# Sliding-window attention and a two-layer MLP on one core: token tiles of 512 instead of 384, with four accumulator banks, the activation kept in PSUM and fixed places for the attention

## The chip, the core and the metric

The kernel runs on one core of a Trainium2 chip. The metric is the device time of one execution in microseconds, as the median of the runs. A core has five engines with a queue each, which this text calls by the profile's names: PE (TensorE, the matrix array; PEld is its loading of weights), DVE (VectorE), ACT (ScalarE), POOL (GpSimd) and SP (SyncE, which here only issues DMAs). SBUF is the working memory of 128 partitions. PSUM is the memory that PE writes; it has eight banks, each holding 512 float32 values in each partition. [...]

## What is computed

```python
def _attn_ref(q, k, v):                    # B, H, S, D = 8, 8, 576, 64
    scores = 1.0 / np.sqrt(D) * np.matmul(q, k.transpose(0, 1, 3, 2))
    rel = pos[:, None] - pos[None, :]
    mask_plain = (rel >= 0) & (rel < 32)                     # heads 0 to 3
    mask_dil = (rel >= 0) & (rel < 128) & (rel % 4 == 0)     # heads 4 to 7
    ...
    attn = softmax of the masked scores
    return np.matmul(attn, v)

def _moe_ref(x, w_in, w_out):              # 4608 tokens, 512 -> 2048 -> 512
    h = x @ w_in
    g = np.where(h >= 1, h, np.where(h <= -1, 0.0, (h + 1) ** 2 / 4))
    return g @ w_out
```

The attention's output, 8 batches of 576 tokens with 8 heads side by side, is the input `x` of the MLP. All data is float32.

## The kernel before

**Precision.** PE multiplies one float32r term by another at one pass. The kernel splits most operands into a high and a low part and adds three products (high by high, low by high, high by low), so each float32 product of the MLP is three matmuls. `xh`/`xl`, `gh`/`gl` and the two halves of `wi` and `wo` are such parts.

**The MLP.** It walks over NT = 12 tiles of TOK = 384 tokens and, in each, over 16 blocks `f` of 128 hidden units. One pair (tile, f) is a step, 192 in all. `layer1(t, f)` runs 12 matmuls (four 128-row chunks of `x` by three terms) of 384 columns into a PSUM tile with the tag `h` (two buffers). Then comes the activation: ACT computes relu(h/2 + 1/2) into `y` in SBUF (L365), DVE multiplies min(y, 1) by y (L366) and takes the maximum with `h` (L367), which is the last reader of `h`; ACT rounds `y` to `gh` (L370), and DVE, or POOL in the first 11 steps of tile 0, computes `gl = y - gh` (L372). `layer2(t, f)` (L385) runs 9 matmuls of 512 columns: three 128-token blocks, each with an accumulator bank `acc0` to `acc2` of its own that is open over all 16 steps, times three terms. After f = 15 the three banks are copied out, two by ACT and one by DVE, and stored.

**The attention.** A query tile is 96 rows and sees 128 keys, six such tiles to a head. The 16 heads of batches 0 and 1 are *native*: `scores` (L187) multiplies unsplit float32, which the trace shows as two matmuls for each query tile, and the heads of a pair lie in partitions 0 to 63 and 64 to 127. `reduce` on DVE (L158) adds the mask and takes the maximum, `softmax` runs six exponentials on ACT (L233), a sum and a reciprocal on DVE (L241, L244) and one multiplication on POOL (L245). `transpose_pe` (L280, L282) turns a native head's weights by PE and copies them out of PSUM, four query tiles by ACT and two by DVE. `values(n, part)` (L313) multiplies a pair of heads by `v` and writes `xh` and `xl` (L298 on ACT, L299 on DVE). The other 48 heads are split: `split` makes high and low parts on ACT and POOL (L134 to L139), `scores_split` (L208) scores two query tiles at a time; ACT copies the low half out of PSUM (L216), POOL adds the mask (L226), and DVE reduces (L158). Their transposes run on DVE (L255).

**Banks.** PSUM's eight banks are `acc0` to `acc2`, two of `h` and three of `att`, which serves scores, transposes and values. While no MLP work runs, batch 0 uses the `acc` and `h` banks too.

**Order.** PE's queue is written out by hand. First all of batch 0's attention runs, then `partial` does the first chunk of layer 1 for `early` = 5 blocks, and then the steps follow: each step `s` issues `layer1(s)`, then `layer2(s - 2)`, and between or behind them units of attention. Over tile 0 these are the eight heads of batch 1 from the list `units`, spread evenly; later `pattern` gives the split heads six steps for each pair, from step 15 on, so 24 pairs fill 144 steps. On the other engines a scheduler orders the instructions by their place in the program, with the priorities raised around batch 0. The weights arrive as 64-bit numbers and are converted while tile 0 runs: two operations on ACT (L111, L117 or on DVE L119), one on DVE (L122), a rounding on ACT (L127) and a subtraction on POOL (L128) for each of 32 blocks; `issue_after` ties their pace to the activation two steps back. Tile 1 needs all of batch 1, so its first step stands behind that batch's attention. DMAs are issued by SP in the order of the program: `load_pair`, `load`, `load_values` and `fetch`.

Of the kernel before, what the change touches and what calls it, by code (L numbers as in the profile page):

```python
# [27 lines left out]
QT, NQ = 96, 6  # L28
KPAD = S + 32
CLS = S // DIL  # L30
TOK = 384
# [8 lines left out]
def body(ctx, tc, q, k, v, mask, eye, w_in, w_out, out):  # L40
# [63 lines left out]
    def weights(f, w, name):  # L104
# [22 lines left out]
        nc.scalar.copy(out=w[f][:, 0], in_=mf)  # L127
# [16 lines left out]
    banks = [("acc0", 1), ("acc1", 1), ("acc2", 1), ("h", 2), ("h", 2)]  # L144
# [24 lines left out]
    def scores(n, t0, t1):  # L169

        hd = heads[n]
        plain = n % H < H // 2
        if t0 == 0:
            begin(n)
        if n < H:
            tag, bufs = banks[(2 * n + t0 // 4) % len(banks)]
        else:
            tag, bufs = "att", 3
        sp = ps.tile([128, 512], F32, tag=tag, name=f"s{n}_{t0}", bufs=bufs)
        sv = sp[:QT, : (t1 - t0) * 128].rearrange("p (t j) -> p t j", j=128)  # L180
        if n == 0 and t0 == 0:

            half = half_t.broadcast_to([128, 128])
            for _ in range(11):
                PE.matmul(out=sp[:, :128], lhsT=half, rhs=half, start=True, stop=True)
        for t in range(t0, t1):
            PE.matmul(  # L187
                out=sv[:, t - t0],
                lhsT=hd["qs"][:, t * QT : (t + 1) * QT],
                rhs=hd["ks"][:, t * QT : t * QT + 128],  # L190
                start=True,
                stop=True,
            )
        for t in range(t0, t1):
            which = (0 if t == 0 else 2) if plain else t % 3
            reduce(n, t, (sv[:, t - t0], msk[:, which]))

    def scores_split(n, t0):
# [6 lines left out]
        sp = ps.tile([128, 512], F32, tag="att", name=f"s{n}_{t0}", bufs=3)  # L205
# [53 lines left out]

    def borrow_pts():  # L260

        for i in range(2):
            for part in ("xh", "xl"):
                both = pool.tile([128, NC * TOK], F32, tag=part, name=f"pts_{part}{i}", bufs=4)
                for j in range(2):
                    pt = both[:, j * NQ * QT : (j + 1) * NQ * QT]
                    first_pts.append(pt.rearrange("p (t j) -> p t j", j=QT))

    first_pts = []

    def pt_of(n):
        return first_pts[n] if n < H else pts[n % 2]

    def transpose_pe(n):
        pt, c = pt_of(n), heads[n]["c"]
        for t0, t1 in ((0, 4), (4, NQ)):
            tag, bufs = banks[(2 * n + t0 // 4) % len(banks)] if n < H else ("att", 3)
# [3 lines left out]
            copy = nc.scalar.copy if t0 == 0 else nc.vector.tensor_copy  # L281
# [4 lines left out]
    def xtile(t):  # L286
        if t not in xt:
            xt[t] = (
                pool.tile([128, NC, TOK], F32R, tag="xh", name=f"xh{t}", bufs=4),
                pool.tile([128, NC, TOK], F32R, tag="xl", name=f"xl{t}", bufs=4),  # L290
            )
        return xt[t]
# [10 lines left out]
    def values(n, part):  # L303

        b, h = divmod(n, H)
        plain = h < H // 2
        odd = b % 2
        first = (2 if odd else 4) if plain else 3
        t0, t1 = ((0, first), (first, NQ))[part]
        op = ps.tile([128, 512], F32, tag="att", name=f"o{n}_{part}", bufs=3)  # L310
        for j in range(2):
            for t in range(t0, t1):
                PE.matmul(  # L313
                    out=op[64 * j : 64 * j + 64, (t - t0) * QT : (t - t0 + 1) * QT],
                    lhsT=heads[n + j]["vt"][:, t],
                    rhs=pt_of(n + j)[:, t],
                    start=True,
                    stop=True,
                )
        c = h // 2  # L320
        tok0 = b * S
        if plain:
            w = (t1 - t0) * QT
            tok = tok0 + t0 * QT
            t, at = divmod(tok, TOK)
            store_x(op[:, :w], t, c, lambda x: x[:, at : at + w])
        else:
            cut = CLS * (TOK // 2 if odd else TOK) // S
            for a, z in ((0, cut), (cut, CLS)):
                t, at = divmod(tok0 + DIL * a, TOK)  # L330
                store_x(
                    op[:, : 2 * CLS].rearrange("p (r i) -> p r i", r=2)[:, :, a:z],
                    t,
                    c,
                    lambda x: x[:, at : at + DIL * (z - a)].rearrange("p (i r) -> p r i", r=DIL)[
                        :, 2 * part : 2 * part + 2
                    ],
                )
# [6 lines left out]
    def layer1(t, f, cs=range(NC), bank=("h", 2)):  # L345
        xh, xl = xtile(t)
        if cs[0] == 0:
            hps[t, f] = ps.tile([128, 512], F32, tag=bank[0], name=f"h{t}_{f}", bufs=bank[1])[:, :TOK]
# [14 lines left out]
        gh = pool.tile([128, TOK], F32R, tag="gh", name=f"gh{t}_{f}", bufs=3)  # L363
        gl = pool.tile([128, TOK], F32R, tag="gl", name=f"gl{t}_{f}", bufs=3)
        nc.scalar.activation(out=y, in_=hp, func=AF.Relu, bias=half_t, scale=0.5)  # L365
        nc.vector.scalar_tensor_tensor(out=y, in0=y, scalar=1.0, in1=y, op0=ALU.min, op1=ALU.mult)  # L366
        activated = nc.vector.tensor_tensor(out=y, in0=hp, in1=y, op=ALU.max)  # L367
        if t == 0:
            last["g", f] = activated
        nc.scalar.copy(out=gh, in_=y)  # L370
        low = nc.gpsimd if t == 0 and f < 11 else nc.vector
        low.tensor_tensor(out=gl, in0=y, in1=gh.bitcast(F32), op=ALU.subtract)  # L372
# [4 lines left out]
    def layer2(t, f):  # L377
        gh, gl = gs.pop((t, f))
        for m in range(TOK // 128):
# [24 lines left out]
    units = []  # L404

    slots = {}

    def plan_rest():

        pattern = [("0", "1"), ("2", "VW"), ("", ""), ("T3", "4"), ("5", ""), ("U", "")]  # L410

        def after(m):
            if m < nhead - 1:
                split(m + 1)
            if m < nhead - 2:
                load(m + 2)
            softmax(m)

        for p in range((nhead - native) // 2 + 1):
            n = native + 2 * p  # L420
            ops = {"V": [lambda n=n: values(n - 2, 0)], "W": [lambda n=n: values(n - 2, 1)]}
            if n < nhead:
                for j in range(2):
                    for i, u in enumerate(score_units(n + j, after)):
                        ops[str(3 * j + i)] = [u]
                ops["T"] = [lambda n=n: (transpose(n), load_values(n))]
                ops["U"] = [lambda n=n: transpose(n + 1)]
            for i, (a, b) in enumerate(pattern):
                if p == 0 and i < 3:
                    continue  # L430
                s = NF + 6 * p + i - 3
                lists = slots.setdefault(s, ([], []))
                for names, l in ((a, lists[0]), (b, lists[1])):
                    for x in names:
# [211 lines left out]
```

## Time and profile before

| what | us |
|---|---|
| median of 3 runs | 976.36 |
| the profiled execution, its own time | 976.49 |
| span of its trace, first to last instruction | 974.7 |
| mean granted TensorE clock over the span | 0.981 |
| DVE busy | 707.2 (73%) |
| ACT busy | 537.5 (55%) |
| POOL busy | 428.7 (44%) |

Of the three runs one took 2337 us and the other two lie 0.16 us apart; the median is one of those two. The profiled execution takes 1.8 us more than its span. A row of groups reads: line, engine, operation, output<-inputs, shape, count | busy us, mean ns of one | idle time of that engine before them, and what ended it. A row of windows reads: the window, its length, and for each engine the time that it is busy and its count of instructions. A row of the timeline or of the chain reads: start, duration (both us), engine, line, tiles, count, and in square brackets the wait in front with what ended it.

### The profile page before, as it was taken

Reading aid. Unit: us, or ns where it says so; the run is one execution under the profiler, and the core shown is the slowest. Engines: PE = TensorE matmul, PEld = TensorE weight load, DVE = VectorE, ACT = ScalarE, POOL = GpSimd, SP = SyncE. Lnnn points to the kernel's source line nnn. Section 1 sums busy time; section 2 is a strip of 40 time slices with the busy share of each in tenths; the row PEclk is TensorE's granted clock in tenths of the full one; section 3 lists DMA queues with packets and bytes.
Section 4 is the critical chain, followed back from the end, with each engine's and each line's share of the span. In section 5 each row is a group of like instructions: output and inputs, shape, how many; then the busy total and the mean of one; then the engine's idle time right before and its main releaser. Section 6 shows DMA issues by size and latency. Waiting matters only on the chain.

```text
span 974.7 us, 15838 instructions
## 1 busy us (share of the span) xinstructions
PE 950.1 (97%) x5398; PEld 847.6 (87%) x5398; DVE 707.2 (73%) x1922; ACT 537.5 (55%) x1609; POOL 428.7 (44%) x375
## 2 busy tenths in 40 slices
PE   8879989999999999999999999999999999999998
PEld 7767778888989888888889888889888888999997
DVE  5688998878777877877787887788777876434433
ACT  6987666555565565556555655654664564322322
POOL 2566665545554554455455445545544551000000
PEclk8689999999999999999999999999999999999999
DMA  8991113113212211321222222212312310000000
GB/s 258 325 377 45 42 42 99 55 54 100 67 36 88 67 58 51 100 67 45 81 67 67 74 68 67 78 48 67 99 43 67 99 34 1 33 1 1 33 1 32
DMA packets 35888, 73.95 MB, mean 76 GB/s; under 512 B 4288, under 2 KB 12768, under 8 KB 35808
## 3 DMA queue, kind: packets, MB, share of 16 engines
q1 hardware_dynamic: 35808, 72.95, 23.7%
q8 instruction: 42, 0.69, 0.3%
q14 instruction: 38, 0.31, 0.1%
HBM read 63.49 MB, written 9.44 MB: 75 GB/s over the span
## 4 chain that ended last, share of the span: by engine, by line
PE 77%; DVE 8%; ACT 6%; DMA 4%; SPq 1%; POOL 1%; issue 1%; POOLq 0%; ACTq 0%; DVEq 0%
PE h L352 36%; PE acc L385 35%; PE o L313 3%; PE s L208 3%; DVE y L366 2%; ACT c L233 2%; DMA wo_raw<-w_in 2%; DVE wo_m L122 1%; DMA kr<-k_in 1%; DVE pt L255 1%; DVE y L367 1%; DVE st L241 1%; ACT y L365 1%; ACT gh L370 1%; DMA vt<-v_in 1%
## 5 line engine op out<-in xcount | busy, mean ns | idle before, releaser
L352 PE MATMUL h<-xh,wi 128*128 128x384 f32 x1536 | 432.9, 343 | 5.2 <-DVE y L367 5.0
L385 PE MATMUL acc<-wo,gh 128*128 128x512 f32 x1152 | 395.2, 397 | 0.8 <-DVE out L395 0.8
L352 PEld LDWEIGHTS h<-xh,wi 128*128 128x128 f32 x1536 | 284.1, 189 | 15.1 <-DVE y L367 5.2
L352 PE MATMUL h<-xl,wi 128*128 128x384 f32 x768 | 261.1, 340 | 0.0
L385 PEld LDWEIGHTS acc<-wo,gh 128*128 128x128 f32 x1152 | 217.8, 189 | 45.2 <-DVE out L395 2.0
L226 POOL TENSOR_TENSOR c<-c,msk 96x256 f32<-96x256 f32 (+1 forms) x168 | 122.9, 737 | 298.7 <-ACT c L216 297.7
L370 ACT CAST gh<-y 128x384 fp32r<-128x384 f32 x192 | 98.1, 511 | 256.4 <-DVE y L367 256.4
L385 PE MATMUL acc<-wo,gl 128*128 128x512 f32 x576 | 228.3, 396 | 0.0
L366 DVE SCALAR_TENSOR_TENSOR y<-y 128x384 f32<-128x384 f32 x192 | 138.3, 720 | 77.2 <-ACT y L365 76.0
L365 ACT ACTIVATE y<-h,half_t 128x384 f32<-128x384 f32 x192 | 111.1, 578 | 135.3 <-PE h L352 135.2
L372 DVE TENSOR_TENSOR gl<-y,gh 128x384 fp32r<-128x384 f32 x181 | 114.0, 630 | 57.0 <-ACT gh L370 55.4
L352 PEld LDWEIGHTS h<-xl,wi 128*128 128x128 f32 x768 | 145.6, 190 | 4.6
L233 ACT ACTIVATE c<-c,st 96x128 f32<-96x128 f32 x348 | 137.0, 395 | 8.6 <-DVE st L158 7.7
L255 DVE STREAM_TRANSPOSE pt<-c 32x192 f32<-32x192 f32 x288 | 106.2, 369 | 24.7 <-POOL c L245 20.6
L385 PEld LDWEIGHTS acc<-wo,gl 128*128 128x128 f32 x576 | 109.1, 189 | 17.3 <-POOL gl L372 0.2
L158 DVE CUSTOM_DVE_ANT_0 c<-s,c 96x128 f32<-96x128 f32 x288 | 73.2, 284 | 61.5 <-POOL c L226 56.2
L367 DVE TENSOR_TENSOR y<-h,y 128x384 f32<-128x384 f32 x192 | 107.0, 558 | 6.5
L245 POOL TENSOR_TENSOR c<-c,st 96x768 f32<-96x768 f32 x58 | 89.5, 1542 | 42.2 <-DVE st L244 35.4
L139 POOL TENSOR_TENSOR kk<-kr,kk 128x608 fp32r<-128x608 f32 x48 | 82.0, 1709 | 3.8
L136 POOL TENSOR_TENSOR qs<-qr,qs 64x576 fp32r<-64x576 f32 x48 | 69.6, 1451 | 5.9 <-issue 2.3
L241 DVE SCALAR_TENSOR_TENSOR st<-st 96x6 f32<-96x6 f32 x58 | 62.5, 1078 | 6.1 <-ACT c L233 5.0
L233 ACT ACTIVATION_READ_ACCUMULATOR c<-c,st 96x1 f32 x348 | 65.9, 190 | 0.0
(53 smaller groups left out, 760.4 us busy)
## 6 DMA issues: line engine op xcount, KB each, us to landing
kr<-k_in SPq DMA_DIRECT2D x48, 304.0 KB, 3.2
qr<-q_in SPq DMA_DIRECT2D x48, 288.0 KB, 2.8
vt<-v_in SPq DMA_DIRECT2D x64, 192.0 KB, 3.1
out<-out SPq DMA_DIRECT2D x36, 256.0 KB, 2.1
wi_raw<-w_in SPq DMA_DIRECT2D x16, 512.0 KB, 9.5
wo_raw<-w_in SPq DMA_DIRECT2D x16, 512.0 KB, 10.5
kr<-k_in SPq DMA_DIRECT2D x16, 152.0 KB, 3.6
qr<-q_in SPq DMA_DIRECT2D x16, 144.0 KB, 3.8
```

Of the source, the lines that this page charges most:

```text
L139: nc.gpsimd.tensor_tensor(out=kk[:, 1], in0=hd["kr"], in1=kk[:, 0].bitcast(F32), op=ALU.subtract)
L226: nc.gpsimd.tensor_tensor(out=c[:, ts], in0=c[:, ts], in1=m, op=ALU.add)
L233: nc.scalar.activation(out=c[:, t], in_=c[:, t], func=AF.Exp, bias=st[:, 0, t : t + 1], scale=-1.0, accum_out=st[:, 1, t : t + 1],)
L245: nc.gpsimd.tensor_tensor(out=c, in0=c, in1=st[:, 2].unsqueeze(2).broadcast_to([QT, NQ, 128]), op=ALU.mult)
L255: nc.vector.transpose(out=pt[r : r + 32, :, 32 * g : 32 * g + 32], in_=c[32 * g : 32 * g + 32, :, r : r + 32],)
L352: PE.matmul(out=hp, lhsT=wi[f][:, w, 128 * c : 128 * c + 128], rhs=x[:, c], start=c == 0 and i == 0, stop=c == NC - 1 and i == len(terms) - 1,
L365: nc.scalar.activation(out=y, in_=hp, func=AF.Relu, bias=half_t, scale=0.5)
L366: nc.vector.scalar_tensor_tensor(out=y, in0=y, scalar=1.0, in1=y, op0=ALU.min, op1=ALU.mult)
L367: activated = nc.vector.tensor_tensor(out=y, in0=hp, in1=y, op=ALU.max)
L370: nc.scalar.copy(out=gh, in_=y)
L372: low.tensor_tensor(out=gl, in0=y, in1=gh.bitcast(F32), op=ALU.subtract)
L385: PE.matmul(out=acc[m], lhsT=g[:, r], rhs=wo[f][:, w], start=f == 0 and i == 0, stop=f == NF - 1 and i == len(terms) - 1,)
```

## The change

- **Tiles.** TOK becomes 512, so there are 9 tiles and 144 steps. A step has 12 matmuls of 512 columns in `layer1` and, with four 128-token blocks, 12 of 512 in `layer2`. `xh` and `xl` have three buffers instead of four, of a third more each.
- **Banks.** `acc0` to `acc3`, two `h`, two `att`. Every odd accumulator is copied out by DVE.
- **Activation.** The maximum is written back into `h`; `gh` and `gl` are both made from there, `gl` always on DVE. `gh` and `gl` have two buffers instead of three.
- **Weights.** The blocks that `convert` handles (wi 0 to 4 and wo 0) are shifted and rounded by DVE instead of ACT.
- **Native heads.** `scores_pair` issues the matmuls of two heads alternately, into two banks. For batch 0 both copies of `transpose_pe` run on DVE.
- **Values.** Both parts of a pair are three query tiles each and run one behind the other.
- **Places.** `place(u, ...)` puts each unit of attention into a half step `u`: 2s lies between `layer1(s)` and `layer2(s - 2)`, 2s + 1 behind it. Batch 1 starts at -2, ahead of `partial`, and ends at 29; the split heads take eight half steps (four steps) for a pair, from 27 (step 13) to 222 (step 111). `early` is 4, in the banks acc2, acc3 and h.

```diff
-TOK = 384
+TOK = 512
...
-    def weights(f, w, name):
+    def weights(f, w, name, on_vector=False):
...
-        if name == "wi":
+        if name == "wi" and not on_vector:
...
-        nc.scalar.copy(out=w[f][:, 0], in_=mf)
+        (nc.vector.tensor_copy if on_vector else nc.scalar.copy)(out=w[f][:, 0], in_=mf)
...
-    banks = [("acc0", 1), ("acc1", 1), ("acc2", 1), ("h", 2), ("h", 2)]
+    banks = [("acc0", 1), ("acc1", 1), ("acc2", 1), ("acc3", 1), ("h", 2), ("h", 2)]
+    turn = [0]
+
+    def bank(n):
+
+        if n >= H:
+            return "att", 2
+        turn[0] += 1
+        return banks[(turn[0] - 1) % len(banks)]
...
+    def scores_pair(n, t0, t1):
...
+            tag, bufs = bank(n)
+            sp = ps.tile([128, 512], F32, tag=tag, name=f"s{m}_{t0}", bufs=bufs)
...
         for t in range(t0, t1):
+            for m, sv in zip(pair, svs):
+                PE.matmul(
+                    out=sv[:, t - t0],
+                    lhsT=heads[m]["qs"][:, t * QT : (t + 1) * QT],
+                    rhs=heads[m]["ks"][:, t * QT : t * QT + 128],
...
-            copy = nc.scalar.copy if t0 == 0 else nc.vector.tensor_copy
+            copy = nc.scalar.copy if t0 == 0 and n >= H else nc.vector.tensor_copy
...
-    def values(n, part):
+    def values(n):
...
+        for part in range(2):
+            op = ps.tile([128, 512], F32, tag="att", name=f"o{n}_{part}", bufs=2)
...
-        gh = pool.tile([128, TOK], F32R, tag="gh", name=f"gh{t}_{f}", bufs=3)
-        gl = pool.tile([128, TOK], F32R, tag="gl", name=f"gl{t}_{f}", bufs=3)
+        gh = pool.tile([128, TOK], F32R, tag="gh", name=f"gh{t}_{f}", bufs=2)
+        gl = pool.tile([128, TOK], F32R, tag="gl", name=f"gl{t}_{f}", bufs=2)
         nc.scalar.activation(out=y, in_=hp, func=AF.Relu, bias=half_t, scale=0.5)
         nc.vector.scalar_tensor_tensor(out=y, in0=y, scalar=1.0, in1=y, op0=ALU.min, op1=ALU.mult)
-        activated = nc.vector.tensor_tensor(out=y, in0=hp, in1=y, op=ALU.max)
+
+        activated = nc.vector.tensor_tensor(out=hp, in0=hp, in1=y, op=ALU.max)
         if t == 0:
             last["g", f] = activated
-        nc.scalar.copy(out=gh, in_=y)
-        low = nc.gpsimd if t == 0 and f < 11 else nc.vector
-        low.tensor_tensor(out=gl, in0=y, in1=gh.bitcast(F32), op=ALU.subtract)
+        nc.scalar.copy(out=gh, in_=hp)
+        nc.vector.tensor_tensor(out=gl, in0=hp, in1=gh.bitcast(F32), op=ALU.subtract)
...
-                if m == 1:
+                if m % 2:
...
+    for n in range(H, native, 2):
+        u = 4 * (n - H) - 2
+        place(u, lambda n=n: scores_pair(n, 0, 4))
+        place(u + 1, lambda n=n: (scores_pair(n, 4, NQ), after_pair(n)))
+        place(u + 5, lambda n=n: transpose_pe(n))
+        place(u + 6, lambda n=n: transpose_pe(n + 1))
+        place(u + 7, lambda n=n: values_native(n))
+    for n in range(native, nhead, 2):
+        u = 27 + 4 * (n - native)
+        for j, at in ((0, u), (1, u + 4)):
+            place(at, lambda m=n + j: scores_split(m, 0))
+            place(at + 1, lambda m=n + j: scores_split(m, 2))
+            place(at + 2, lambda m=n + j: (scores_split(m, 4), after(m)))
+        place(u + 4, lambda n=n: (transpose(n), load_values(n)))
+        place(u + 8, lambda n=n: transpose(n + 1))
+        place(u + 11, lambda n=n: values(n))
...
-    early = len(banks)
+
+    early_banks = [("acc2", 1), ("acc3", 1), ("h", 2), ("h", 2)]
+    early = len(early_banks)
...
+        run(-2)
         partial(range(1))
+        run(-1)
         convert(("wo", 0), ("wi", early))
...
+            run(2 * s)
+            while l2 <= s - lag and l2 < len(steps):
+                layer2(*steps[l2])
                 l2 += 1
...
+            run(2 * s + 1)
```

More of the change, by code (lines that the diff above doesn't have):

```diff
@@ L167, in reduce @@
         )
-    def scores(n, t0, t1):
-        hd = heads[n]
+    def scores_pair(n, t0, t1):
+        pair = (n, n + 1)
         plain = n % H < H // 2
[L173 to L185, printed above, removed]
-        for t in range(t0, t1):
[L187 to L196, printed above, removed]
+        svs = []
+        for m in pair:
+            if t0 == 0:
+                begin(m)
+            tag, bufs = bank(n)
+            sp = ps.tile([128, 512], F32, tag=tag, name=f"s{m}_{t0}", bufs=bufs)
+            svs.append(sp[:QT, : (t1 - t0) * 128].rearrange("p (t j) -> p t j", j=128))
+            if m == 0 and t0 == 0:
+                half = half_t.broadcast_to([128, 128])
+                for _ in range(11):
+                    PE.matmul(out=sp[:, :128], lhsT=half, rhs=half, start=True, stop=True)
+        for t in range(t0, t1):
+            for m, sv in zip(pair, svs):
[3 more added lines that the diff above has]
+                    rhs=heads[m]["ks"][:, t * QT : t * QT + 128],
+                    start=True,
+                    stop=True,
+                )
+        for m, sv in zip(pair, svs):
+            for t in range(t0, t1):
+                which = (0 if t == 0 else 2) if plain else t % 3
+                reduce(m, t, (sv[:, t - t0], msk[:, which]))
     def scores_split(n, t0):
@@ L301, in store_x @@
         )
-    def values(n, part):
+    def values(n):
         b, h = divmod(n, H)
         plain = h < H // 2
[L307 to L338, printed above, removed]
@@ L402, in body @@
     native = 2 * H
-    units = []
     slots = {}
[L408 to L434, printed above, removed]
-                        if not (p == 0 and x in "VW012"):
-                            l.extend(ops.get(x, []))
@@ L438, in score_units, with place @@
[L438 to L465 removed]
+    def place(u, *ops):
+        slots.setdefault(u, []).extend(ops)
@@ L466, in after_first, with after_pair, after @@
+    def after_pair(n):
+        softmax(n)
+        softmax(n + 1)
+        if n + 4 < native:
+            load_pair(n + 4)
+        elif n + 4 == native:
+            load(native)
+        else:
+            split(native)
+            load(native + 1)
+    def after(m):
+        if m < nhead - 1:
             split(m + 1)
+        if m < nhead - 2:
             load(m + 2)
-            softmax(m)
-        units.extend(score_units(native, after_first))
-        units.append(lambda: transpose_pe(native - 1))
@@ L517, in early_values, with run @@
         with tc.high_priority(offset=150):
-            values(n, 0)
-            values(n, 1)
+            values(n)
     def partial(cs):
         for f in range(early):
-            layer1(0, f, cs, ("att", 3) if f == 2 else banks[f])
+            layer1(0, f, cs, early_banks[f])
     def convert(*blocks):
         for name, f in blocks:
-            weights(f, {"wi": wi, "wo": wo}[name], name)
+            weights(f, {"wi": wi, "wo": wo}[name], name, True)
+    def run(u):
+        for op in slots.pop(u, ()):
+            op()
     with tc.manual_schedule(engines={mybir.EngineType.PE}):
-        for n in range(0, H, 2):
-            pair(n)
+        pair(0)
+        pair(2)
+        pair(4)
+        pair(6)
         early_transposes(0)
```

131 lines of the change are left out of this document (54 added, 77 removed).

## The prediction, made before the changed kernel ran

> **What bounds the kernel now.** I read the page first: which engine is busy, where in the span, and what the chain of waits ends on.
>
> ```profile
> span 974.7 us, 15838 instructions
> PE 950.1 (97%) x5398; PEld 847.6 (87%) x5398; DVE 707.2 (73%) x1922; ACT 537.5 (55%) x1609; POOL 428.7 (44%) x375
> DVE  5688998878777877877787887788777876434433
> PE 77%; DVE 8%; ACT 6%; DMA 4%; SPq 1%; POOL 1%; issue 1%; POOLq 0%; ACTq 0%; DVEq 0%
> ```
>
> PE is the bound, but the chain gives it 77%, not 97%: the rest, on DVE, ACT and DMA, must lie where DVE's slices (of 24.4 us) are fullest, in the third to sixth, 49 to 146 us. So I read the chain at both ends of the span.
>
> ```profile
> 68.59 4.21 PE h L352 x12
> ...
> 153.33 2.31 PE h L352 x12
> ```
>
> ```profile
> 836.75 2.11 PE h L352 x12
> 838.85 2.08 PE acc L385 x9
> ...
> 962.69 2.12 PE h L352 x12
> 964.81 6.17 PE acc L385 x27
> ```
>
> The second fence is the MLP alone. From 836.75 to 962.69 lie 30 steps, so a step is 4.198 us: 12 matmuls of 384 columns in 2.11 (176 ns each) and 9 of 512 in 2.09 (232 ns each). The durations of 340 to 400 ns in the rows of groups overlap and are no price. The windows then divide the span.
>
> ```profile
> 42.20:153.00 110.80, 99.39 (x563) 83.40 (x563) 97.59 (x227) 82.91 (x233) 72.76 (x55) 0.92 0.39 136
> 585.00:682.00 97.00, 97.00 (x550) 87.11 (x549) 76.23 (x210) 53.81 (x167) 51.48 (x45) 1.00 0.22 65
> 829.00:877.00 48.00, 48.00 (x243) 43.62 (x242) 19.97 (x36) 13.56 (x26) 0.00 (x0) 1.00 0.05 17
> ```
>
> In order the columns are PE, PEld, DVE, ACT, POOL (busy us), clock, DMA share and GB/s. From 153 us on PE never stands still and DVE has a quarter to spare. From 42.2 (the first matmul of layer 1) to 153 DVE is busy 88%. Who waits there? The same window for four lines of PE (L352, L187, L280, L313 in this order; the first number is PE's), and PE's waits from 42 to 150:
>
> ```profile
> 42.20:153.00 110.80, 41.75 (x192) 36.49 (x192) 0.92 0.39 136
> 42.20:153.00 110.80, 13.53 (x96) 10.95 (x96) 0.92 0.39 136
> 42.20:153.00 110.80, 7.13 (x48) 5.51 (x48) 0.92 0.39 136
> 42.20:153.00 110.80, 6.43 (x95) 5.43 (x95) 0.92 0.39 136
> ```
>
> ```profile
> PE h L352 <- DVE y L367: 5.0, 1, 5.0
> PE t L280 <- DVE xl L299: 2.5, 2, 1.8
> PE t L280 <- DVE st L158: 2.3, 2, 2.1
> ```
>
> The 192 matmuls of L352 are 16 steps of 12: this stage is exactly tile 0. At full speed its PE work is 16 x 2.11 + 14 x 2.09 for the MLP, 13.5 for native scores, 7.1 for transposes and 6.4 for values, together 90. The stage takes 111. The other 21 are waits, nearly all on DVE, and the slow clock behind them: the 12 matmuls at 68.59, after the wait of 5.0, took 4.21 instead of 2.11. So there are two kernels in one: tile 0, which DVE paces, and the rest, which PE paces.
>
> **The change part by part.**
>
> *Steps of 512.* At 232 ns a matmul, a step is 24 x 0.232 = 5.568 us. The MLP's 192 x 4.198 = 806.0 becomes 144 x 5.568 = 801.8: minus 4. Larger matmuls bring no more than that, since both sizes already cost nearly the same for a column (0.458 and 0.453 ns).
>
> *Behind tile 0.* Before, PE runs from 153.3 to 964.81 + 6.17 = 971.0, that is 817.7. Of this 176 steps take 738.8 and two more halves of layer 2 take 4.2; the remaining 74.7 is attention. It stays the same: same instructions, same switches. After: 128 x 5.568 + 2 x 2.784 + 74.7 = 793.0, and 3.7 from the last matmul to the end (974.7 - 971.0). So the new span is T + 796.7, with T the start of tile 1; at T = 178 nothing is gained.
>
> *Cover behind tile 0.* A pair of heads (3.1 us of attention, 74.7 / 24) now has four steps, 4 x 5.568 + 3.1 = 25.4 us, where six took 28.3. DVE's work for a pair was 78.6% of that (76.23 of 97), 22.2; in it 18 instructions of the MLP at some 0.56 become 12 at 0.68 (rows below), 1.9 less. 20.3 of 25.4 is 80%; ACT and POOL have more room. The banks are the question. These rows are the timeline around one pair:
>
> ```profile
> 600.85 1.43 PE L313 MATMUL o<-pt,vt 128*64 128x96 f32 x24
> ...
> 604.25 0.34 PE L352 MATMUL h<-xh,wi 128*128 128x384 f32 x1
> ...
> 605.21 0.91 DVE L299 TENSOR_TENSOR xl<-o,xh 128x192 fp32r<-128x192 f32 x2 [0.34 <-ACT xh L298]
> 605.32 0.56 ACT L365 ACTIVATE y<-h,half_t 128x384 f32<-128x384 f32 x1
> ...
> 608.62 0.40 PE L208 MATMUL s<-kk,qs 128*96 128x256 f32 x2
> ...
> 610.14 0.56 DVE L372 TENSOR_TENSOR gl<-y,gh 128x384 fp32r<-128x384 f32 x1 [0.58 <-ACT gh L370]
> ...
> 612.04 0.28 DVE L158 CUSTOM_DVE_ANT_0 c<-s,c 96x128 f32<-96x128 f32 x1
> ```
>
> A bank of scores is taken at 608.62 and free at 612.3: 3.7 us. With two `att` banks the tightest place is the values of a pair, one half step behind the third score unit: its second part needs that unit's bank after 0.2 for the scores, 2.8 for half a step and 0.7 for the first part, also 3.7. The wait is therefore between 0 and 1.6 us for each of 24 pairs (1.6 if DVE is as late as in the values at 600.85, whose banks were free only at 606.1, 5.3 behind); I take 0, since the nearest row, of scores, fits, and keep the other end for a rival. `h` is now held until `gl`: layer 1 ended at 604.6, `gl` at 610.7, 6.1 us, to which larger instructions add some 0.5; it is needed again two halves of layer 2 and one of layer 1 later, 8.4. Covered by 1.8. Two buffers of `gh` make ACT's rounding wait for the end of `layer2(s - 2)`, 2.8 us behind layer 1, where it could start after some 2.1 (0.7 + 2 x 0.68); ACT is 55% busy, what queues behind (exponentials) has its slack of several steps, and the `gl` that follows still comes before 8.4: nothing. Copies of `acc` (two by DVE now), the moved DMAs of `load`, `load_values` and `load_pair` on SP (DMA share 0.22) and three `x` buffers of 512 (the same bytes as four of 384) cost nothing under the same cover; if it goes, each is a wait of PE of its own length once in a tile.
>
> *Tile 0.* PE's work becomes 30 x 2.784 = 83.5 for the MLP, 7.1, 6.4, and less for the native scores:
>
> ```profile
> 5.84 4.59 PE L187 MATMUL s<-kr,qr 64*96 64x128 f32 x48
> ```
>
> ```profile
> 107.82 1.55 PE L187 MATMUL s<-kr,qr 64*96 64x128 f32 x12
> ```
>
> One head alone takes 129 ns for a matmul; in the first row, where heads of both halves of the partitions follow each other, 96. Issued alternately they may overlap fully (half, 6.8) or not at all (13.5); I take 8.5, nearer to the overlap that the first row shows in part. Sum 105.5. With the 21 of waits and slow clock as before, T = 42.2 + 105.5 + 21 = 169; with 5 left, 153.
>
> DVE decides between these. Its groups from 42 to 150, then from 840 to 960, where POOL is idle:
>
> ```profile
> L366 DVE SCALAR_TENSOR_TENSOR y<-y 128x384 f32<-128x384 f32 x15 | 25.5, 1698 | 5.4 <-ACT y L365 5.3
> L122 DVE SCALAR_TENSOR_TENSOR wo_m<-wo_m,wo_raw 128x512 uint32<-128x512 uint32 x16 | 21.4, 1343 | 0.9 <-ACT wo_m L111 0.9
> L372 POOL TENSOR_TENSOR gl<-y,gh 128x384 fp32r<-128x384 f32 x11 | 12.2, 1107 | 8.7 <-ACT gh L370 5.4 <-issue 3.4
> L122 DVE SCALAR_TENSOR_TENSOR wi_m<-wi_m,wi_raw 128x512 uint32<-128x512 uint32 x13 | 11.3, 869 | 1.1 <-ACT wi_m L111 1.1
> L372 DVE TENSOR_TENSOR gl<-y,gh 128x384 fp32r<-128x384 f32 x4 | 3.5, 874 | 0.0
> ```
>
> ```profile
> L366 DVE SCALAR_TENSOR_TENSOR y<-y 128x384 f32<-128x384 f32 x29 | 16.2, 559 | 55.4 <-ACT y L365 55.4
> L367 DVE TENSOR_TENSOR y<-h,y 128x384 f32<-128x384 f32 x29 | 16.2, 557 | 1.0
> L395 DVE COPY out<-acc 128x512 f32<-128x512 f32 x2 | 1.4, 679 | 0.0
> ```
>
> L366 costs 559 ns with POOL idle and 1698 beside it. At 512 columns an undisturbed instruction costs about 680 (L395), 120 more than at 384. So tile 0 adds 16 x 0.12 twice (L366, L367), 3.9; `gl` is 16 x 0.68 = 10.9 instead of 3.5, plus 7.4; rounding and shifting of wi 4 and wo 0 add 1.5 (those of wi 0 to 3 and the copies of batch 0's transposes lie ahead of 42, where DVE's first two slices are 5 and 6 tenths full). Against it POOL loses 12.2 of its 72.8: 17% of what contention costs, 16 x 1.14 + 16 x 0.66 + 13 x 0.19 = 31, so minus 5 (0 if the stalls come from the weights alone). DVE: 97.6 + 3.9 + 7.4 + 1.5 - 5 = 105.4, and at 88% that is 119.8: T = 162; without the 5 it is 168. I take 162, between PE's ends of 153 and 169, since DVE's busy share is what the rows show directly.
>
> [...]
>
> *Start.* The first pair of batch 1 now stands ahead of `partial` and needs both `att` banks, which the last values hold:
>
> ```profile
> 40.68 1.57 PE L313 MATMUL o<-pts_xl,vt 128*64 128x96 f32 x12 [1.21 <-DVE xl L299]
> ```
>
> ```profile
> 47.59 0.34 DVE L299 TENSOR_TENSOR xl<-o,xh 128x96 fp32r<-128x96 f32 x1
> ```
>
> The last `xl` ended at 47.9, 5.7 us behind those values, so PE may stand still for 0 to 5.7 us. I add nothing, as DVE sets T and works meanwhile; the 5.7 is in the upper end.
>
> *Sum.* Span 162 + 796.7 = 958.7. The profiled execution takes 1.8 us more than its span (976.49), and lies 0.1 above the median of 976.36: 960.5.
>
> **The rivals.** *PE paces tile 0:* with `gl` off POOL, DVE's contention falls by more than a sixth, and 5 us of waits remain: T = 153, 951.5. For it: L366 loses twice its own price to POOL. Against: DVE was 88% busy and gets more work.
>
> *Tile 0 loses what it gains:* with two `att` banks each native unit waits for the reductions or copies of the one before, in DVE's fullest stage; some 16 such places at 0.5 us over the 21 give T = 42.2 + 105.5 + 29 = 177, 975, no change. For it: the waits of 1.8 and 2.1 above are of this kind, with three banks, and a long one doubles the price of what follows, as at 68.59. [...]
>
> *Slower:* the two `att` banks make PE wait in every pair behind tile 0. Each microsecond costs 24. It decides from (995.9 - 960.5) / 24 = 1.5 us a pair; at 2 us the time is 1008. For it: the values at 600.85 held their banks for 5.3 us. Against: scores fit the 3.7 that there are, so DVE's queue must grow by 1.5 us, at a load of 80% as before.
>
> **How the numbers follow.** Forecast 46%, PE paces 26%, gain lost 16%, slower 12%. The forecast's own range is T from 154 to 171, 952 to 970. For 8 in 10 the range reaches over PE's pace and the lost gain, 946 to 982; the slower case and the edges stay outside. About 2% is what a measurement of this kernel can tell from no change: faster means below 956.8, slower above 995.9. Faster: the PE case and a tenth of the forecast, 0.31. Slower: 0.12. Same: 0.57.
>
> **What would show it.** Tile 1's first matmul of layer 1 near 162; L352 at 232 ns a matmul; a step of 5.57 in the tail; L372 near 680 ns whether or not POOL is busy; L366 in tile 0 below 1.8 us; native scores at 5 to 9 us in that window; and behind tile 0 no wait of PE on L158 or L299. The prediction is wrong if PE waits for `att` behind tile 0 by more than 10 us in total, if T is below 154 or above 171, or if a 512-column matmul of layer 1 does not cost what layer 2's does.

## The result, and the profile after

The changed kernel takes 992.94 us (median of four runs, 990.98 to 993.14), the kernel before 976.30 on the same chip (also four runs, one of them the run of 2337 us, which the ratio leaves out): ratio 1.0166, 95% interval 1.0146 to 1.0186. It became 1.7% slower. That is within the 2% called no change, but outside the predicted range of 946 to 982 and on the other side of 976.36 than the forecast of 960.5.

First the head of the page of the changed kernel: the span, each engine's busy time, DVE's 40 slices (now of 24.8 us) and the shares of the chain that ended last.

```profile
span 991.4 us, 14524 instructions
...
PE 940.7 (95%) x4822; PEld 752.6 (76%) x4822; DVE 661.9 (67%) x1830; ACT 515.8 (52%) x1504; POOL 413.3 (42%) x364
...
DVE  5978876776677777777777777767776643334333
...
DVE 38%; PE 26%; ACT 24%; issue 5%; POOL 4%; SPq 2%; DMA 1%; POOLq 0%; ACTq 0%; DVEq 0%
```

The busy shares would say that little happened: PE has 95% instead of 97%. The chain says much more. Before, 77% of it lay on PE; now 26%, with 38% on DVE and 24% on ACT. So PE is kept waiting again and again by small amounts for as long as there is attention. The chain's last pieces, where only the MLP runs, show that the matmuls are not to blame:

```profile
970.28 2.81 PE h L360 x12
973.09 2.76 PE acc L393 x12
975.84 2.81 PE h L360 x12
```

A step is 975.84 - 970.28 = 5.56 us, as the prediction had it (5.568). The windows divide the span as before: tile 0, a tile in the middle, and the MLP alone. The first row is tile 0, from the first matmul of layer 1 to tile 1. Its bounds come from my own table of the records, which counts 0.2 to 0.3 us less than the page; by the page's rows tile 0 runs from 54.56 to 168.22.

```profile
54.30:168.00 113.70, 107.93 (x593) 84.56 (x592) 87.42 (x232) 80.55 (x220) 55.14 (x40) 0.96 0.30 94
592.60:698.80 106.20, 102.60 (x529) 81.68 (x529) 77.72 (x225) 59.97 (x185) 57.42 (x52) 1.00 0.24 73
840.00:888.00 48.00, 48.00 (x208) 38.84 (x207) 18.73 (x27) 10.80 (x17) 0.00 (x0) 1.00 0.00 0
```

Before, PE was busy for all 97 us of the middle window. Now it stands still for 3.6 of 106.2. Set beside the prediction's sum, by the page's rows:

| piece, us | forecast | measured |
|---|---|---|
| first matmul of layer 1 | 42.2 | 54.6 |
| tile 0 from there | 119.8 | 113.7 |
| start of tile 1 (T) | 162 | 168.2 |
| from there to the end | 796.7 | 991.4 - 168.2 = 823.2 |
| span | 958.7 | 991.4 |

Of the 32.7 us too many, 6.2 lie ahead of tile 1 and 26.5 behind it. These are PE's largest waits:

```profile
PE s L217 <- POOL kk L139: 11.9, 22, 1.1
PE s L217 <- DVE xl L307: 9.5, 12, 1.5
PE o L322 <- issue: 8.2, 2, 5.6
```

**Behind tile 0.** From the trace I took PE's start-to-start intervals by what follows what. Only one kind is dear: from a matmul of layer 2 to scores, in 80 places of 20 pairs (168.0 to 698.8), 40.6 us in all, where an undisturbed interval is 0.231 (the median; 0.232 in the kernel before), 18.5 in all. The excess is 22.1 us, 1.1 for a pair. Counted on from T to the last pair it is 25.2 us (46.7 in 93 places, against 21.5): nearly all of the 26.5. The timeline shows where the longer of the two chains behind it comes from. In the changed kernel, between the last scores of one head and the first of the next:

```profile
598.58 0.40 PE L217 MATMUL s<-kk,qs 128*96 128x256 f32 x2
...
600.58 0.68 ACT L134 CAST qs<-qr 128x576 fp32r<-128x576 f32 x1
...
600.76 0.74 POOL L235 TENSOR_TENSOR c<-c,msk 96x256 f32<-96x256 f32 x1 [2.07 <-ACT c L225]
...
601.16 0.70 ACT L135 CAST kk<-kr 128x608 fp32r<-128x608 f32 x1
...
601.58 1.42 POOL L136 TENSOR_TENSOR qs<-qr,qs 64x576 fp32r<-64x576 f32 x1
...
603.08 1.93 POOL L139 TENSOR_TENSOR kk<-kr,kk 128x608 fp32r<-128x608 f32 x1
...
605.06 0.48 PE L217 MATMUL s<-kk,qs 128*96 128x256 f32 x2 [0.55 <-POOL kk L139]
```

`qs` and `kk` have one buffer each, so `split` of the next head cannot begin before the last scores of this one have been read. From there two casts on ACT, a mask and two subtractions on POOL follow each other, and `kk` is ready at 603.08 + 1.93 = 605.01. The first cast starts 1.60 us behind the end of the scores (598.98), since ACT has two exponentials, `gh` and a copy to do first. PE wanted `kk` at 605.06 - 0.55 = 604.51. The same place in the kernel before:

```profile
598.45 0.40 PE L208 MATMUL s<-kk,qs 128*96 128x256 f32 x2
...
599.44 0.68 ACT L134 CAST qs<-qr 128x576 fp32r<-128x576 f32 x1
...
602.49 1.69 POOL L139 TENSOR_TENSOR kk<-kr,kk 128x608 fp32r<-128x608 f32 x1
```

There the chain took 5.7 us (598.45 to 604.18; the first cast came 0.59 us behind the scores), and the next scores came at 608.62 (a row of the prediction): 4.4 to spare. In the changed kernel `after` stands at u + 2 and the next head's scores at u + 4, two half steps on: 5.9 us by these rows, where the chain took 6.4.

**The start.** PE's rows in the changed kernel, from the first values to the first matmul of layer 1, with three rows of DVE:

```profile
25.23 2.40 PE L322 MATMUL o<-pts_xh,vt 128*64 128x96 f32 x24
...
34.49 0.74 DVE L307 TENSOR_TENSOR xl<-o,xh 128x288 fp32r<-128x288 f32 x2
...
35.03 0.71 PE L322 MATMUL o<-pts_xh,vt 128*64 128x96 f32 x3 [5.65 <-issue]
...
46.32 2.54 PE L322 MATMUL o<-pt,vt 128*64 128x96 f32 x24 [2.53 <-issue]
...
50.75 0.21 DVE L307 TENSOR_TENSOR xl<-o,xh 128x32 fp32r<-128x32 f32 x1 [0.93 <-ACT xh L306]
...
51.06 0.71 PE L195 MATMUL s<-kr,qr 64*96 64x128 f32 x2 [2.20 <-issue]
...
52.33 0.21 DVE L307 TENSOR_TENSOR xl<-o,xh 128x32 fp32r<-128x32 f32 x1 [0.46 <-ACT xh L306]
...
52.64 1.99 PE L195 MATMUL s<-kr,qr 64*96 64x128 f32 x14 [0.87 <-issue]
...
54.56 0.79 PE L360 MATMUL h<-xh,wi 128*128 128x512 f32 x1
```

Both parts of a pair's values now take the two `att` banks, so the next pair waits until DVE has made the last pair's `xl`, 5.65 us at 35.03; the heads of batch 1, ahead of `partial`, wait in the same way. Each of the four pieces that waited starts 0.10 us behind the end of an `xl` (34.93, 46.22, 50.96 and 52.54). The four waits are 11.2 us. Ahead of layer 1 PE stands idle for 20.5 of 54.6 us, where in the kernel before it was 8.7 of 42.2, so nearly all of the 12.4 us by which layer 1 starts late is waiting.

**Tile 0.** It is shorter than forecast, and DVE's groups from 54 to 165 say why:

```profile
L374 DVE SCALAR_TENSOR_TENSOR y<-y 128x512 f32<-128x512 f32 x15 | 13.3, 886 | 5.5 <-ACT y L373 5.4
L122 DVE SCALAR_TENSOR_TENSOR wo_m<-wo_m,wo_raw 128x512 uint32<-128x512 uint32 x13 | 12.1, 930 | 0.7
L376 DVE TENSOR_TENSOR h<-h,y 128x512 f32<-128x512 f32 x15 | 10.5, 698 | 0.4
...
L380 DVE TENSOR_TENSOR gl<-h,gh 128x512 fp32r<-128x512 f32 x15 | 10.2, 682 | 1.7 <-ACT gh L379 1.7
```

The multiplication that took 1698 ns (there L366) takes 886 although it is a third larger.

### The profile page after: what moved, and what is told of

It is laid out like the page before. It is cut to its first block, busy times and chain, and to the rows that moved or that the text cites. A ratio compares the mean times of both kernels' runs of the same rounds, so it can differ in the third digit from the quotient of the medians.

```text
span 991.4 us, 14524 instructions
## 1 busy us (share of the span) xinstructions
PE 940.7 (95%) x4822; PEld 752.6 (76%) x4822; DVE 661.9 (67%) x1830; ACT 515.8 (52%) x1504; POOL 413.3 (42%) x364
## 4 chain that ended last, share of the span: by engine, by line
DVE 38%; PE 26%; ACT 24%; issue 5%; POOL 4%; SPq 2%; DMA 1%; POOLq 0%; ACTq 0%; DVEq 0%
PE h L360 13%; PE acc L393 12%; ACT c L242 10%; DVE pt L264 10%; DVE y L374 9%; DVE h L376 6%; ACT y L373 4%; DVE st L250 3%; ACT kk L135 3%; ACT gh L379 3%; ACT qs L134 3%; DVE xl L307 3%; POOL c L254 3%; DVE c L166 2%; DVE gl L380 2%
## 5 line engine op out<-in xcount | busy, mean ns | idle before, releaser
L360 PE MATMUL h<-xh,wi 128*128 128x512 f32 x1152 | 387.7, 397 | 0.0
L393 PE MATMUL acc<-wo,gh 128*128 128x512 f32 x1152 | 386.9, 397 | 0.0
L393 PEld LDWEIGHTS acc<-wo,gh 128*128 128x128 f32 x1152 | 217.2, 189 | 50.4
L360 PEld LDWEIGHTS h<-xh,wi 128*128 128x128 f32 x1152 | 217.5, 189 | 48.3 <-issue 0.3
L360 PE MATMUL h<-xl,wi 128*128 128x512 f32 x576 | 227.8, 396 | 0.0
L393 PE MATMUL acc<-wo,gl 128*128 128x512 f32 x576 | 227.2, 395 | 0.2 <-DVE gl L380 0.2
L374 DVE SCALAR_TENSOR_TENSOR y<-y 128x512 f32<-128x512 f32 x144 | 128.7, 894 | 124.7 <-ACT y L373 121.8
L380 DVE TENSOR_TENSOR gl<-h,gh 128x512 fp32r<-128x512 f32 x144 | 99.4, 690 | 107.4 <-ACT gh L379 106.6
L373 ACT ACTIVATE y<-h,half_t 128x512 f32<-128x512 f32 x144 | 97.8, 679 | 113.9 <-PE h L360 113.8
L379 ACT CAST gh<-h 128x512 fp32r<-128x512 f32 x144 | 83.5, 580 | 135.7 <-PE acc L393 73.3
L393 PEld LDWEIGHTS acc<-wo,gl 128*128 128x128 f32 x576 | 108.6, 189 | 22.2 <-DVE gl L380 0.5
L360 PEld LDWEIGHTS h<-xl,wi 128*128 128x128 f32 x576 | 108.9, 189 | 21.0
L376 DVE TENSOR_TENSOR h<-h,y 128x512 f32<-128x512 f32 x144 | 100.0, 695 | 3.1
L217 PE MATMUL s<-kk,qs 128*96 128x256 f32 x288 | 60.0, 289 | 24.2 <-POOL kk L139 11.9
L217 PEld LDWEIGHTS s<-kk,qs 128*96 128x96 f32 x288 | 43.3, 161 | 51.1 <-POOL kk L139 21.3
L139 POOL TENSOR_TENSOR kk<-kr,kk 128x608 fp32r<-128x608 f32 x48 | 78.7, 1639 | 3.8
```

Of the source, the lines that this page charges most:

```text
L217: PE.matmul(out=sv[:, t - t0], lhsT=hd["qs"][:, t * QT : (t + 1) * QT], rhs=hd["ks"][:, :, t * QT : t * QT + 128], start=True, stop=True,)
L360: PE.matmul(out=hp, lhsT=wi[f][:, w, 128 * c : 128 * c + 128], rhs=x[:, c], start=c == 0 and i == 0, stop=c == NC - 1 and i == len(terms) - 1,
L376: activated = nc.vector.tensor_tensor(out=hp, in0=hp, in1=y, op=ALU.max)
L379: nc.scalar.copy(out=gh, in_=hp)
L380: nc.vector.tensor_tensor(out=gl, in0=hp, in1=gh.bitcast(F32), op=ALU.subtract)
L393: PE.matmul(out=acc[m], lhsT=g[:, r], rhs=wo[f][:, w], start=f == 0 and i == 0, stop=f == NF - 1 and i == len(terms) - 1,)
```

## The experiments

The expectations count the span by first and last instruction in my own table of the records, which is 0.2 to 0.3 us below the page's; so do the starts of layer 1 and of tile 1 (T) in this section, where the changed kernel has 54.3 and 168.0. Runs without an interval are single ones beside the kernel before on the same chip, which took 974.9 to 975.7 there.

**1. The activation in PSUM, put into the kernel before** (tiles of 384, three `att` banks).

```diff
-        activated = nc.vector.tensor_tensor(out=y, in0=hp, in1=y, op=ALU.max)
+        activated = nc.vector.tensor_tensor(out=hp, in0=hp, in1=y, op=ALU.max)
...
-        nc.scalar.copy(out=gh, in_=y)
-        low = nc.gpsimd if t == 0 and f < 11 else nc.vector
-        low.tensor_tensor(out=gl, in0=y, in1=gh.bitcast(F32), op=ALU.subtract)
+        nc.scalar.copy(out=gh, in_=hp)
+        nc.vector.tensor_tensor(out=gl, in0=hp, in1=gh.bitcast(F32), op=ALU.subtract)
```

> The kernel before with only the activation's change: the maximum is written into h in PSUM, gh and gl are made from there, gl always by DVE. Theory (in tile 0 DVE loses its time to POOL, and gl on POOL is what holds it): L366 falls from 1.70 us beside POOL to below 1.0, the first matmul of tile 1 moves from 153 us to 138 to 144, and the time falls to 961 to 968. Rival (the shorter stage of the changed kernel comes from steps of 512, or from the lighter native units): L366 stays above 1.4 us, tile 1 starts after 150 and the time stays within 972 to 980. Behind tile 0 neither expects a wait of PE.

Measured: 967.44 us against 975.20, ratio 0.9918 (0.9902 to 0.9935). T is 144.6 instead of 153.0 (just behind the 138 to 144 expected), so the whole gain lies in tile 0. This kernel is faster than both, if by only 0.8% against the kernel before (its interval leaves out 1). Its groups of DVE from 42 to 145:

```profile
L366 DVE SCALAR_TENSOR_TENSOR y<-y 128x384 f32<-128x384 f32 x16 | 12.2, 762 | 6.1 <-ACT y L365 5.8
...
L371 DVE TENSOR_TENSOR gl<-h,gh 128x384 fp32r<-128x384 f32 x16 | 8.6, 540 | 0.0
```

**2. Only `gl` moved to DVE, in the kernel before**; it is still made from `y` in SBUF.

```diff
-        low = nc.gpsimd if t == 0 and f < 11 else nc.vector
-        low.tensor_tensor(out=gl, in0=y, in1=gh.bitcast(F32), op=ALU.subtract)
+        nc.vector.tensor_tensor(out=gl, in0=y, in1=gh.bitcast(F32), op=ALU.subtract)
```

> The kernel before with gl always on DVE, but still made from y in SBUF. If taking gl off POOL is what counts, L366 falls below 1.0 us as in the run before this, and tile 1 starts by 146. If reading from PSUM is what counts (an input from PSUM is not held up by POOL), gl itself costs over 1.2 us in tile 0 and tile 1 starts after 148.

Measured: 967.25, T 143.8. The gain is the same, so it comes from taking `gl` off POOL and not from PSUM. The same two groups, from 42 to 144, differ from those of experiment 1:

```profile
L371 DVE TENSOR_TENSOR gl<-y,gh 128x384 fp32r<-128x384 f32 x16 | 15.8, 990 | 0.2 <-ACT gh L370 0.2
L366 DVE SCALAR_TENSOR_TENSOR y<-y 128x384 f32<-128x384 f32 x16 | 15.3, 954 | 4.6 <-ACT y L365 4.5
```

With both inputs in SBUF `gl` takes 990 ns beside POOL, with one of them in PSUM 540. These 10 us of DVE's time in the two groups move T by nothing. DVE's busy time in tile 0 as a whole rises by only 3.2 us (93.7 instead of 90.5), as other groups take less. So T did not follow DVE's load here, but the difference in load is too small to settle what sets the length of tile 0.

**3. The changed kernel with the activation as before**, `gl` on POOL in 11 steps (experiment 1's diff the other way round).

> The changed kernel with the activation as before: y in SBUF, gl on POOL in the first 11 steps. If the activation is what made tile 0 short: L374 rises from 0.89 us in tile 0 to above 1.4, tile 1 starts at 176 to 184 instead of 168, and the time is 1000 to 1010. Rival (the schedule of tile 0 alone): tile 1 starts within 166 to 171.

Measured: 1009.32, T 176.2 instead of 168.0, and 8 us more behind tile 0 (831.1 against 823.2, by the page's rows). The multiplication, from 53 to 176:

```profile
L374 DVE SCALAR_TENSOR_TENSOR y<-y 128x512 f32<-128x512 f32 x16 | 19.5, 1218 | 5.4 <-ACT y L373 5.4
```

It rose, though not above the 1.4 us expected. So this part of the change is worth some 16 us to it. The rest of the change lost more than that. Over 20 pairs behind tile 0 the intervals from layer 2 to scores are 2.9 us longer and those inside the values 3.8; which of the edited instructions brings this was not separated.

**4. The early conversions and batch 0's first copies back on ACT, in the changed kernel.**

```diff
-            weights(f, {"wi": wi, "wo": wo}[name], name, True)
+            weights(f, {"wi": wi, "wo": wo}[name], name)
...
-            copy = nc.scalar.copy if t0 == 0 and n >= H else nc.vector.tensor_copy
+            copy = nc.scalar.copy if t0 == 0 else nc.vector.tensor_copy
```

> The changed kernel with the early conversions and batch 0's copies back on ACT. Theory (DVE's conversions stand ahead of xl, which holds the att banks): layer 1 starts at 45 to 49 us instead of 54.3, and the time falls by as much. Rival (the two att banks alone, or the pair ahead of partial): layer 1 starts after 51.

Measured: 992.63, layer 1 from 53.5, T 167.7. The theory that DVE's added work at the start delays layer 1 falls. Without it the second pair's values do begin earlier, at 29.56 instead of 35.03, but PE then waits 3.23, 4.05 and 3.30 us further on (at 34.36, 45.30 and 51.14), and layer 1 comes only 0.8 us earlier.

**5. Batch 0's values in the free banks** (`acc`, `h`), in the changed kernel.

```diff
-            op = ps.tile([128, 512], F32, tag="att", name=f"o{n}_{part}", bufs=2)
+            tag, bufs = bank(n) if n < 6 else ("att", 2)
+            op = ps.tile([128, 512], F32, tag=tag, name=f"o{n}_{part}", bufs=bufs)
```

> The changed kernel with the values of heads 0 to 5 in the turning acc and h banks, which stand free then, instead of the two att banks. Theory (the values of batch 0 wait for each other's xl, since two banks are too few while DVE's queue is long): the wait of 5.6 us before the second pair's values goes, layer 1 starts at 45 to 50 us instead of 54.3, and the time falls by that. Rival (the pair of batch 1 ahead of partial holds it): layer 1 still starts after 52.

Measured: 989.84, layer 1 from 47.8, T 164.6. The start moves as expected, the time falls by less (3.1 us). The wait before the second pair's values did not go: it is still 4.01 us, at 32.88, again 0.10 behind the end of an `xl`, since the turn of six banks comes back there to the two of the first pair. Of the four waits shown above, those of 2.53 and 0.87 us are gone.

**6. The same, and `partial` ahead of batch 1's first heads.**

```diff
-        run(-2)
         partial(range(1))
+        run(-2)
         run(-1)
```

> The run before this, and partial ahead of the first pair of batch 1. Theory of both parts: layer 1 starts at 41 to 45 us, as in the kernel before (42), and the time is 982 to 987 against 993. If only the banks count, it starts as in the run before this, less the pair's own 2 us.

Measured: 987.26, layer 1 from 43.5, T 162.6, span 985.5. The time is just above the 982 to 987 expected. The two edits bring 6.5 and 4.3 us of start (in the second figure 1.1 are the first 16 scores of batch 1 themselves), so both kinds of wait for the two `att` banks are real. Of 10.8 us of earlier start 5.4 reach T; tile 0 becomes longer, 119.1 instead of 113.7. Of that, 1.1 are these 16 scores, which now lie inside it. Where the other 4.3 go was not separated.

**7. Two `att` banks in the kernel before**, nothing else: `bufs=3` becomes 2 at the tag `att`.

> The kernel before with two att banks instead of three and nothing else changed. Theory (the third bank is what the attention needs at any tile size): layer 1 starts later than 42 by 3 us or more, PE waits for L299 or L158 behind tile 0 by over 10 us in total, and the time is over 990. Rival (it is the eight half steps for a pair that are too close): layer 1 may start late, but behind tile 0 PE waits for under 4 us in total, and the time stays below 984.

Measured: 994.04 against 974.94. T is 160.9 (7.9 later), and a tile of 384 takes 76.5 instead of 75.5 us (mean of the nine tiles behind tile 0). The third bank alone is worth 19 us to the kernel before. Behind tile 0 it is 9.7 us, of which 8.6 lie inside the values (38.9 us over 24 pairs instead of 30.3); PE's listed waits there for L158 and L299 are 5.2 us, not over 10 as expected.

**8. The low part of `kk` on DVE, in the changed kernel.**

```diff
-        nc.gpsimd.tensor_tensor(out=kk[:, 1], in0=hd["kr"], in1=kk[:, 0].bitcast(F32), op=ALU.subtract)
+        nc.vector.tensor_tensor(out=kk[:, 1], in0=hd["kr"], in1=kk[:, 0].bitcast(F32), op=ALU.subtract)
```

> The changed kernel with the low part of kk made by DVE instead of POOL, beside the low part of qs. Theory (a head's first scores wait for its split, which may begin only behind the scores of the head before and runs through ACT and twice through POOL in two half steps): the 11.9 us of PE's waits on L139 fall below 3 and the time by 8 to 12. Rival (PE would wait there for the att banks anyway): the waits move to L307 or L166 and the time falls by less than 4.

Measured: 983.68, span 981.9, T 168.8: 9.5 us less, all behind tile 0. PE's waits for `kk` are gone, those of L217 for `xl` fell from 9.5 to 1.7, and the intervals from layer 2 to scores sum to 20.4 us, near the undisturbed 18.5. Why the waits for `xl` fell too was not separated: the edit shortens the chain, and it also takes 48 instructions (78.7 us) off POOL. A new wait took part of the gain back, and heads the list:

```profile
PE o L322 <- DVE st L166: 7.8, 16, 0.9
```

It is the second part of a pair's values, which needs the bank of the third score unit. The intervals inside the values rose from 25.7 to 37.6 us over 20 pairs, 0.6 for a pair.

**9. Both repairs**, 6 and 8 together, in the changed kernel.

> Both repairs at once. Theory: the late start and the wait for the low part of kk are separate losses, so their gains add: the start gave 5.9 us of span (991.1 to 985.2) and the low part on DVE 9.4 (991.1 to 981.7), together 15.3: span 975.8, time 978, level with the kernel before; tile 1 starts near 163. Rival: both act through DVE's queue, and what the one frees the other uses up: span 980 to 982, time 982 to 984.

Measured: 977.55 against 975.67 (ratio 1.0016, 1.0007 to 1.0026), span 975.9, T 162.0. The span fell by 15.5, the single repairs brought 5.9 and 9.5. The gains add, so the late start and the chain through `kk` are separate losses. By the page's rows what is left of the 26.5 behind tile 0 is 975.9 - 162.2 - 796.7 = 17.0. Of this the intervals inside the values make 13.1 (43.9 us over all 24 pairs instead of 30.8).

**10. The second part of the values half a step later**, on top of 9.

```diff
-    def values(n):
+    def values(n, parts=(0, 1)):
...
-        for part in range(2):
+        for part in parts:
...
-        place(u + 11, lambda n=n: values(n))
+        place(u + 11, lambda n=n: values(n, (0,)))
+        place(u + 12, lambda n=n: values(n, (1,)))
```

> Both repairs, and the second part of a pair's values half a step behind the first instead of right behind it. Theory: what is left behind tile 0 is that second part waiting for the bank of the third score unit; the intervals inside the values sum to 37.7 us over 20 pairs where the changed kernel had 25.7, so 0.6 us a pair or 14.4 for 24 pairs should go: span 975.9 - 14.4 = 961.5, time 963.4, below both kernels. Rival: with two banks the wait only moves on, to the score unit that now follows the second part: span 970 to 976, time 972 to 978.

Measured: 994.52 against 975.68 (ratio 1.0198, 1.0178 to 1.0218), T 162.4. My theory falls, and the rival is right in kind though its loss was put too low. Over 20 pairs the intervals inside the values fell from 37.7 to 27.4 us, but the scores behind layer 1 now wait, 21.6 us over 40 places where 9.3 is undisturbed, layer 1 itself is 3.7 us longer, and the matmuls' changes of kind, of which there are more, cost 4.0. PE's two largest waits:

```profile
PE s L217 <- DVE xl L307: 7.9, 13, 1.5
PE s L217 <- DVE st L166: 6.0, 7, 1.6
```

So this move only moved the wait, to a neighbour half a step away that wants the same bank; whether some other order fits two banks was not tried. Nor was a second buffer for `qs` and `kk`, which would take the other chain apart.

**11. Native heads one behind the other**, in the changed kernel: the two loops of `scores_pair` change places.

```diff
-        for t in range(t0, t1):
-            for m, sv in zip(pair, svs):
+        for m, sv in zip(pair, svs):
+            for t in range(t0, t1):
```

> The changed kernel with the two native heads scored one behind the other instead of alternately; L195 should go from 7.5 us in tile 0 to some 13.5. Theory: in the changed kernel PE paces tile 0 (busy 107.9 of 113.7 us), so the 6 us show in full: tile 1 starts near 174, time 998 to 999. Rival, the prediction's own view: DVE sets that stage's length, PE's extra time lies in its waits: tile 1 stays at 168, time 993.

Measured: 996.50, tile 0 from 53.8 to 171.1, 3.6 us longer. It is neither of the two, since the edit changed PE's work by little: the 96 matmuls take 11.0 us of PE instead of 9.8 (13.5 in the kernel before). The start times in the trace show why, as differences in ns:

```
before,          one head, 12 matmuls:  187 109 109 109 109 109 110 109 109 109 109
changed,         both heads, 16:        7 180 6 103 6 103 7 102 7 102 7 102 7 103 6
loops exchanged, both heads, 8:         13 174 13 96 13 96 13
```

In the units shown, two heads in different halves of the partitions start in pairs, 6 or 7 ns apart and a pair every 109, when they take turns; in the short units of 8 they start in pairs, 13 ns apart, even when they are issued one behind the other. In the long units of 16 the exchanged loops leave most of them single, 109 apart. Of the 3.7 us that the change saves, 2.5 come from standing side by side in one unit (13.5 to 11.0) and 1.2 from taking turns (11.0 to 9.8). The run does not settle what paces tile 0: of the 3.6 us PE's busy time makes 1.3 (109.3 instead of 107.9), and the rest are waits.

## Why the prediction was wrong

**"It stays the same"** (behind tile 0, 796.7 with covers at nothing) is the step that failed, and it cost 26.5 of the 32.7 us. The MLP's own part of it is right: a step of 5.56, `gl` at 682 ns with POOL busy, no wait for `h` among PE's largest, and ACT's rounding waits for layer 2, as foreseen. PE shows no harm from it (its idle time before L360 is 0.0 and before L393 0.2 us), but no run gave `gh` a third buffer, so whether it delays what stands behind it on ACT is open. Its row among the page's groups of the changed kernel (the last figures are ACT's idle time before it and what ended most of it):

```profile
L379 ACT CAST gh<-h 128x512 fp32r<-128x512 f32 x144 | 83.5, 580 | 135.7 <-PE acc L393 73.3
```

What failed is the search for what is tight. Under "The banks are the question" I measured how long the banks are held and looked, for `att`, at one place, the second part of the values; in the changed kernel its wait is zero (25.7 us over 20 pairs against 26.6 over 21 before). It comes when the chain is shortened: 0.6 us a pair in experiment 8, inside the 0 to 1.6 of which I took 0. I did not ask the same of the other buffers that the new places bring closer: `qs` and `kk`, which are made again for each head. Four steps instead of six for a pair leave two half steps for `split`; 598.45 to 604.18 in the kernel before already showed a chain of 5.7 us beside 5.57 for two half steps of PE. Removing a part of this chain gave 9.5 us (experiment 8). Of the three signs that I gave for being wrong none came up: PE's listed waits for `att` behind tile 0 are 8.0 us (under the 10 named, though I had expected none), T is 168.2, and a matmul costs the same in both layers. They asked about banks, the length of tile 0 and the price of a matmul, not about the buffers in SBUF.

**The slower rival** had the kind of loss right and was given 0.12. It put the point from which it decides at 1.5 us a pair; measured are 1.1. Half of its mechanism holds: the scores behind a pair's values wait for `xl` (9.5 us listed), and two banks alone slow the kernel before (experiment 7). But these waits fall to 1.7 with the banks as they are once DVE makes the low part of `kk` (experiment 8), so they are not the banks' alone. The other half is the chain above, which runs through SBUF and not through `att`.

**"I add nothing, as DVE sets T"** (the start) failed as well. My bound of 0 to 5.7 saw the wait of batch 1's first pair only; the values of batch 0 wait for the two banks too, and layer 1 starts 12.4 us late. The reason given for nothing was half right: of 10.8 us won back, 5.4 reached T.

**"17% of what contention costs"** was mis-sized. The 12.2 us of `gl` on POOL were taken as that share of POOL's work and priced at 5 us. L366 alone lost 1139 ns each to POOL before; L374 loses 194 now (886 against 692 in the last tile, where POOL is idle). In the kernel before, the same step made L366 762 ns and brought 8.4 us of T (experiment 1; 954 ns and 9.2 us in experiment 2). DVE's work in tile 0, forecast as 105.4 us, was 87.4. So tile 0 came out at 113.7 instead of 119.8 and hid half of the late start. With the start repaired (experiment 9) T is 162.2 by the page's rows, the figure forecast, but by luck: there tile 0 takes 118.3 us with DVE busy for 95.1 (80%), not 105.4 at 88%. In the changed kernel PE was busy 107.9 of tile 0's 113.7 us and DVE 77% of it. This looks like the rival "PE paces tile 0", though no run settles what paces that stage.

**Right:** the step; the native scores within the 5 to 9 us named (7.5 us for the 82 of 96 matmuls that lie in the window; all 96 took 9.8, where 8.5 was taken); L374 below 1.8 us; `gl` near 680 ns whether or not POOL is busy (L380, which reads `h` in PSUM, took 682 in tile 0 and 691 from 890 to 975, where POOL is idle; L374, with both inputs in SBUF, took 692 there); and the sum of the repaired parts.

## What to carry to other kernels

When a schedule is made tighter, list every buffer with one or two copies that the moved work writes, banks and SBUF alike, and for each set the time from its last reader to its next use against the chain that fills it, taken from rows of the old trace; a single place that fits says nothing of the others. A resource that is given up (here a bank of PSUM) should be taken from the old kernel alone as a test: that run (experiment 7) showed 19 us at once. And take a change apart before judging it: one of its parts, alone in the kernel before, is worth 8 us.

## What the runs showed of the hardware

Where L366, with both inputs in SBUF, took long in the kernel before, it ended just behind the end of an instruction of POOL: all 29 of its 192 that took over 0.9 us ended 0.41 or 0.42 us behind one. One of them, beside four instructions of POOL:

```profile
75.53 1.77 POOL L245 TENSOR_TENSOR c<-c,st 96x768 f32<-96x768 f32 x1 [3.40 <-ACT wi_raw L117]
75.89 4.02 DVE L366 SCALAR_TENSOR_TENSOR y<-y 128x384 f32<-128x384 f32 x1
...
77.26 1.00 POOL L372 TENSOR_TENSOR gl<-y,gh 128x384 fp32r<-128x384 f32 x1
...
78.23 1.26 POOL L128 TENSOR_TENSOR wo<-wo_m,wo 128x512 fp32r<-128x512 f32 x1
...
79.46 1.60 POOL L128 TENSOR_TENSOR wi<-wi_m,wi 128x512 fp32r<-128x512 f32 x1
```

Where POOL is idle (840 to 960) L366 took 0.56 us. Here it ended at 75.89 + 4.02 = 79.91, 0.42 behind the end of POOL's third instruction (78.23 + 1.26 = 79.49): it lasted past the ends of three in a row, and the fourth was running when it ended. Eleven of the 29 are among tile 0's 16, six of them behind a second or third in a row. At 512 columns, in the changed kernel, the distance is 0.55: all six L374 of tile 0 that took over 0.75 us ended 0.546 to 0.549 us behind the end of an instruction of POOL. With one input in PSUM no such stretch shows: in the changed kernel from 54 to 165 the 15 L376 took 690 to 700 ns and the 15 L380 675 to 693, where the 15 L374, from SBUF alone, took 646 to 1812; in the kernel before from 42 to 153 the 16 L367 took 545 to 559 and the 16 L366 514 to 4022. `gl` took 540 ns on average with an input in PSUM (experiment 1) and 990 from SBUF (experiment 2). So in these traces what L366 lost was not in proportion to POOL's work: with `gl`, 17% of POOL's work in that stage, moved to DVE, its mean fell from 1698 ns to 954 (experiment 2).
